# Attention and a gated MLP on one core: the second MLP product by Strassen's scheme

## Chip, core and metric

The kernel runs on one core of a Trainium2 chip. The metric is the device time of one execution in microseconds (us); lower is better. A core has five engines with a queue each, which work in order and wait for one another by semaphores: PE (TensorE, matmuls from SBUF into PSUM; its weight loads, PEld, overlap the matmuls), ACT (ScalarE), DVE (VectorE), POOL (GpSimd, which has no access to PSUM) and SP (SyncE, which here only issues DMAs). PSUM has eight banks of 512 f32 columns for 128 partitions.

## What is computed

```python
def _attn_ref(q, k, v, g_q, g_k):            # (8, 12, 448, 64) each
    ...
    q_n, k_n = (rmsnorm(q, g_q), rmsnorm(k, g_k))
    scores = scale * np.matmul(q_n, k_n.transpose(0, 1, 3, 2))
    ...
    return np.matmul(attn, v).astype(np.float32)

def _moe_ref(x, w_in, w_out):                # x: (3584, 768)
    h = x @ w_in                             # 768 -> 2048
    relu6 = np.clip(h + 3.0, 0.0, 6.0)
    g = h * relu6 / 6.0
    return (g @ w_out).astype(np.float32)    # 2048 -> 768
```

Eight sequences of 448 tokens and 12 heads go through attention with normalised queries and keys; the heads of a token, side by side, are the 768 inputs of an MLP with a gate, without residual. Inputs and output are f32, the matmuls work on bf16.

## The kernel before

**Units.** Two heads make a pair, so there are 48 pairs, six to a sequence. For a pair P, `load` brings q, k and v into slots of SBUF (slots for q and k: a ring of 6 and 2 that are used once, in space that a later stage takes over; for v likewise 6 and 2). `prep` squares q and k (ACT or POOL), sums the squares (DVE, line 454), takes the inverse root (ACT, lines 430 and 433), scales q and k into bf16 (POOL, line 369), and copies v to bf16 (`values`, on POOL, ACT or DVE). `trans` turns q and k by a DMA on SP's queue (line 561), for the first pairs on PE. `score` makes the scores on PE (line 594) and their exponentials on ACT (line 600), `av` the product with v (line 680), `finish` divides by the row sums (DVE, lines 696 and 699) and turns the result into `xT` by a DMA on SP's queue (line 706).

**The MLP.** When a sequence's six pairs are through, `h_group` computes 128 of the 2048 hidden columns of its 448 tokens: six matmuls of 448 columns (line 772), then on ACT a relu into `ts` (line 731), and on DVE the gate, which reads `ts` and PSUM and writes a row of `gT` in bf16 (line 734). `gT` holds the hidden values with the hidden index on partitions: two buffers of two sequences each (`gT_r`), so that one group of two sequences can be read while the next is written. `y_group` computes 128 tokens of the output: for each half of 384 output columns 16 matmuls that use a block of `gT` as weights and a row block of `w_out_sb` as the moving operand (line 794), all into one PSUM bank, then a copy into a row of the ring `y` (ACT, line 350, or DVE, line 352) and the store (SP's queue, line 815). Two sequences make seven such token tiles; in all there are 28, each 32 matmuls. The last tile's second half is computed in two quarters, so that its copies and stores overlap.

**PSUM.** Two tiles `S` of two banks and a tile `X` of two banks serve the scores and attention; the two banks `M` alternate for `h_group` and `y_group`. Only when attention is over do the MLP's groups get five banks.

**Order.** The program is first written down as a list of steps (`Plan.add`: what kind, which engines may do it, what it reads and writes). `ORDER` is a fixed list that says in which order the steps are issued, and `WAY` says for single steps which of their possible engines does them (0, the first, unless named). `mix` decides only which tiles of the output go beside which hidden columns, and `ORDER` then places every step. In each engine's queue the steps run in that order, whatever comes late.

Of the kernel before, what the change touches and what calls it, by code (L numbers as in the profile page):

```python
# [12 lines left out]
A_MIN = mybir.AluOpType.min  # L13
LN = mybir.ActivationFunctionType.Ln
# [152 lines left out]
]  # L167


# [36 lines left out]
def kernel(  # L206
# [11 lines left out]
    nc = tc.nc  # L218
# [743 lines left out]
```

## Time and profile before

| | |
|---|---|
| times of three runs | 422.86, 424.26, 471.55 us, median 424.26 |
| span of the profiled execution | 421.4 us |
| busiest engine | PE 413.0 us |
| other engines, busy | ACT 288.3, DVE 233.1, POOL 168.8 us |
| mean granted clock of PE | 0.999 |
| HBM read, written | 50.23 MB, 11.01 MB |

The span runs from the first to the last instruction of one execution. A group row of the profile reads: line, engine, operation, what it writes <- what it reads (partitions x elements and type), the count, then busy us and the mean ns of one, then the idle time of the engine just before these instructions and what ended it. Matmuls are pipelined: their durations overlap, and their spacing has to be read from the starts in the timeline. Some matmul records are missing from a trace (here the page shows 3959, the program has 3960).

### The profile page before, as it was taken

How to read it: one execution, taken by the hardware profiler on the slowest of the kernel's cores; microseconds unless marked ns; L12 is line 12 of the kernel's file. 1: busy time of each engine (PE TensorE's matmuls, PEld its weight loads, DVE VectorE, ACT ScalarE, POOL GpSimd, SP SyncE). 2: the span in 40 equal slices, each digit the busy share in tenths (PEclk: the TensorE clock that was granted, in tenths of full speed). 3: DMA queues.
4: the chain of work that ended last, by engine and by line, in shares of the span. 5: the costliest groups of instructions: out<-in, count | busy, mean ns of one | idle time of the engine just before them, and what ended most of it. 6: DMA issues, size and time to landing. Idle time of an engine off the chain costs nothing.

```text
span 421.4 us, 9981 instructions
## 1 busy us (share of the span) xinstructions
PE 413.0 (98%) x3959; PEld 243.8 (58%) x3960; DVE 233.1 (55%) x474; ACT 288.3 (68%) x527; POOL 168.8 (40%) x189
## 2 busy tenths in 40 slices
PE   7899999999999999999999999999999999999996
PEld 3566886555545555555555555555655556555565
DVE  5987776588875667536554754447345333333210
ACT  6999887678887988788767876677765662133201
POOL 3999596478374554427344143043210100000000
PEclk9999999999999999999999999999999999999999
DMA  7999999999779799568495683747350601120034
GB/s 241 319 282 196 258 216 177 275 268 271 178 194 252 193 252 242 111 154 211 115 224 160 164 206 73 135 154 166 82 93 12 143 2 47 30 81 27 8 107 114
DMA packets 98979, 67.77 MB, mean 161 GB/s; under 512 B 53204, under 2 KB 95476, under 8 KB 98932
## 3 DMA queue, kind: packets, MB, share of 16 engines
q1 hardware_dynamic: 93296, 60.50, 56.9%
q0 software_dynamic: 5248, 6.29, 9.0%
q8 instruction: 31, 0.51, 0.5%
q10 hardware_dynamic: 388, 0.34, 0.3%
q14 instruction: 16, 0.13, 0.1%
HBM read 50.23 MB, written 11.01 MB: 145 GB/s over the span
## 4 chain that ended last, share of the span: by engine, by line
PE 82%; DMA 7%; ACT 5%; DVE 2%; issue 1%; POOL 1%; SPq 1%; POOLq 0%; ACTq 0%; DVEq 0%
PE M L772 27%; PE M L794 25%; PE X L680 9%; PE S L594 5%; PE M L753 4%; DMA qk<-in_k_dram 4%; PE S L794 4%; PE X L594 3%; DMA T<-qks 2%; PE X L772 1%; ACT sq L364 1%; DMA out_dram<-y 1%; ACT eT L600 1%; ACT eT L622 1%; PE S L617 1%
## 5 line engine op out<-in xcount | busy, mean ns | idle before, releaser
L794 PE MATMUL M<-w_out_sb,gT 128*128 128x384 bf16 x752 | 139.3, 326 | 0.2 <-DMA w_out_sb<-in_moe_w_out_dram 0.2
L772 PE MATMUL M<-xT,w_in_sb 128*128 128x448 bf16 x618 | 135.0, 353 | 0.1
L369 POOL TENSOR_TENSOR qks<-qk,rs 112x512 bf16<-112x512 f32 (+1 forms) x91 | 91.0, 1019 | 107.3 <-ACT rs L433 77.2
L794 PEld LDWEIGHTS <-gT 128*128 128x128 bf16 x912 | 84.5, 98 | 59.5 <-issue 7.6
L734 DVE SCALAR_TENSOR_TENSOR gT<-ts,M 128x448 bf16<-128x448 f32 x119 | 73.2, 616 | 72.1 <-ACT ts L731 71.6
L600 ACT ACTIVATE eT<-S 112x896 bf16<-112x896 f32 x112 | 100.3, 915 | 15.7 <-PE S L594 8.5
L731 ACT ACTIVATE ts<-M 128x448 f32<-128x448 f32 x119 | 64.7, 545 | 42.7 <-PE M L772 29.2
L772 PEld LDWEIGHTS <-w_in_sb 128*128 128x128 bf16 x672 | 60.2, 98 | 56.3 <-issue 10.5
L366 POOL TENSOR_TENSOR sq<-qk 112x512 f32<-112x512 f32 (+1 forms) x57 | 58.0, 1024 | 52.9 <-DMA qk<-in_q_dram 29.7
L680 PEld LDWEIGHTS <-eT 112*128 112x128 bf16 x1344 | 52.7, 97 | 14.5 <-issue 2.0
L600 ACT ACTIVATE eT<-X 112x896 bf16<-112x896 f32 x56 | 51.3, 917 | 13.3 <-PE X L594 12.2
L680 PE MATMUL X<-va,eT 112*128 112x65 bf16 x1344 | 56.0, 194 | 0.1
L454 DVE TENSOR_REDUCE ssq<-sq 112x16 f32<-112x1024 f32 x42 | 50.9, 1213 | 6.1 <-POOL sq L366 4.7
L594 PE MATMUL S<-T 64*128 64x448 bf16 x224 | 34.0, 353 | 0.1
L352 DVE COPY y<-M 128x384 f32<-128x384 f32 x26 | 14.5, 556 | 30.9 <-PE M L794 30.8
L699 DVE TENSOR_TENSOR xn<-X,rd 112x512 bf16<-112x512 f32 x42 | 28.9, 689 | 1.3 <-DVE rd L696 0.2
L696 DVE RECIPROCAL rd<-X 112x8 f32<-112x8 f32 x42 | 8.6, 206 | 34.5 <-PE X L680 28.6
L594 PEld LDWEIGHTS <-T 64*128 64x128 bf16 x336 | 12.9, 94 | 24.5 <-issue 17.2
L364 ACT ACTIVATE sq<-qk 112x512 f32<-112x512 f32 (+1 forms) x40 | 23.0, 586 | 2.8 <-DMA qk<-in_k_dram 2.5
L350 ACT COPY y<-M 128x384 f32<-128x384 f32 x21 | 10.0, 477 | 19.4 <-PE M L794 19.2
L753 PE MATMUL M<-xT,w_in_sb 128*128 128x224 bf16 x192 | 22.9, 259 | 0.0
L794 PE MATMUL S<-w_out_sb,gT 128*128 128x384 bf16 (+1 forms) x128 | 22.6, 316 | 0.0
(87 smaller groups left out, 300.9 us busy)
## 6 DMA issues: line engine op xcount, KB each, us to landing
qk<-in_k_dram SPq DMA_DIRECT2D x45, 256.0 KB, 4.8
qk<-in_q_dram SPq DMA_DIRECT2D x45, 256.0 KB, 4.7
vf<-in_v_dram SPq DMA_DIRECT2D x43, 256.0 KB, 4.8
w_in_sb<-in_moe_w_in_dram POOLq DMA_DIRECT2D x4, 768.0 KB, 8.4
w_out_sb<-in_moe_w_out_dram POOLq DMA_DIRECT2D x4, 768.0 KB, 9.5
out_dram<-y SPq DMA_DIRECT2D x7, 336.0 KB, 3.5
out_dram<-y SPq DMA_DIRECT2D x8, 288.0 KB, 3.3
out_dram<-y SPq DMA_DIRECT2D x8, 240.0 KB, 2.8
```

Of the source, the lines that this page charges most:

```text
L366: em(nc.gpsimd.tensor_tensor(out=out, in0=in_, in1=in_, op=A_MULT))
L369: em((nc.vector if e == DVE else nc.gpsimd).tensor_tensor(out=out, in0=in_, in1=by.unsqueeze(3).to_broadcast(list(in_.shape)), op=A_MULT))
L454: em(nc.vector.tensor_reduce(out=ssq[:].rearrange("p i n -> p (i n)"), in_=sq[:].rearrange("p i (n d) -> p (i n) d", d=D), axis=AX_X, op=A ...
L594: em(nc.tensor.matmul(out=ps[:, a, 0:S], lhsT=qkT[r, S + t * TP:S + t * TP + 128], rhs=qkT[r, 0:S], start=True, stop=True))
L600: em(nc.scalar.activation(out=eT[:, t, 0:S2].rearrange("p (a s) -> p a s", a=2), in_=ps[0:TP, :, 0:S], func=EXP, bias=0.0, scale=1.0))
L680: em(nc.tensor.matmul(out=X_ps[:, a, i * E1:(i + 1) * E1], lhsT=eT[:, t, c:c + 128], rhs=va[:, a, t, :], start=(t == 0 and i == 0), stop=( ...
L699: em(nc.vector.tensor_tensor(out=xn[:].rearrange("p i a d -> p a i d"), in0=view()[:, :, :, 0:D], in1=rd[:].unsqueeze(3).to_broadcast([TP, ...
L731: em(nc.scalar.activation(out=ts[:], in_=ps()[:, 0:S], func=RELU, bias=0.5, scale=1.0 / 6.0))
L734: em(nc.vector.scalar_tensor_tensor(out=out, in0=shape(ts[:]), scalar=1.0, in1=shape(ps()[:, 0:S]), op0=A_MIN, op1=A_MULT))
L753: em(nc.tensor.matmul(out=ps()[:, f * SH:(f + 1) * SH], lhsT=w_in_sb[:, kt, f0:f0 + 128], rhs=xT[:, kt, z * SH:(z + 1) * SH], start=(kt == ...
L772: em(nc.tensor.matmul(out=ps()[:, 0:S], lhsT=w_in_sb[:, kt, f * 128:(f + 1) * 128], rhs=xT[:, kt, :], start=(kt == 0), stop=(kt == NKT - 1)))
L794: em(nc.tensor.matmul(out=ps()[:, 0:nc0], lhsT=gT[:, f, i * 128:(i + 1) * 128], rhs=w_out_sb[:, f, c0:c0 + nc0], start=(f == 0), stop=(f = ...
```

## The change

The output product is taken by Strassen's scheme for all token tiles from the fourth on. Two token tiles (rows i1, i2), the two halves of the 2048 hidden values and the two halves of the 768 output columns make a 2 x 2 by 2 x 2 product of blocks. Each block product is 8 matmuls of 384 columns. With A for the blocks of `gT` and B for those of `w_out`, `y_pair` forms seven products:

```diff
+    def y_pair(g, i1, i2, nb):
+        row1, row2 = y_row(False), y_row(True)
+        c11, c12, c21, c22 = half(row1, 0), half(row1, 1), half(row2, 0), half(row2, 1)
+        k = [bank(nb), bank(nb)]
+        a6 = gsum(g, 0, (i2, 0), (i1, 0), A_SUB, None)
+        a7 = gsum(g, 1, (i1, 1), (i2, 1), A_SUB, None)
+        a11, a22 = raw(g, i1, 0), raw(g, i2, 1)
+        product(k[0], (a11, B12))
+        y_copy(c22, k[0])
+        product(k[1], (a22, B21))
+        y_add(c22, k[1])
+        a5 = gsum(g, (i1, 1), (i1, 0), (i1, 1), A_ADD, None)
+        a2 = gsum(g, (i2, 0), (i2, 0), (i2, 1), A_ADD, None)
+        product(k[0], (a5, B22), start=False)
+        y_copy(c12, k[0])
+        product(k[1], (a2, B11), start=False)
+        y_copy(c21, k[1])
+        aS = gsum(g, (i1, 0), (i1, 0), (i2, 1), A_ADD, None)
+        yield 4
+        k = bank(nb)
+        product(k, (aS, BSUM))
+        y_add(c22, k)
+        y_sub(c11, c22, c12)
+        y_sub(c22, c22, c21)
+        yield 1
+        k = bank(nb)
+        product(k, (a7, B7))
+        y_add(c11, k)
+        y_store(g, i1, row1, (0, DM))
+        yield 1
+        k = bank(nb)
+        product(k, (a6, B6))
+        y_add(c22, k)
+        y_store(g, i2, row2, (0, DM))
+        yield 1
```

`gsum` is one addition or subtraction of 128 x 1024 bf16 on DVE or POOL, into one of two buffers `ga` or in place over rows of `gT`. `y_add` adds a PSUM product to half a row of y (DVE), `y_sub` subtracts two halves in SBUF (POOL or DVE), `product` is 8 matmuls. With `start=False` a product goes on in a bank that still holds the former one, after that has been copied or added out. There are 11 pairs. The first three tiles stay as they were (`y_plain`), three tiles without a partner (`y_single`) take 32 matmuls and one `gsum`.

`wsums` forms, once, three sums of blocks of `w_out` in a new tensor `wb` and replaces two blocks of `w_out_sb` by differences, in ten steps of 128 x 1536 bf16 on DVE or POOL:

```diff
+            for n, (o, x, y, op, reads, writes) in enumerate((
+                    (wb[:, 1, lo], b11, b12, A_ADD, [rl], [("wb", 1, j)] + OVER_W),
+                    (wb[:, 2, lo], b21, b22, A_ADD, [rh], [("wb", 2, j)] + OVER_W),
+                    (b12, b12, b22, A_SUB, [rl, rh, ("wb", 1, j)], [("w12", j)]),
+                    (b21, b21, b11, A_SUB, [rl, rh, ("wb", 2, j)], [("w21", j)]),
+                    (wb[:, 0, lo], b11, b22, A_ADD, [rl, rh], [("wb", 0, j)] + OVER_W))):
```

For the space, `gT` becomes one tensor of three sequences instead of two buffers of two, with the odd sequences in the middle, and the rings of input slots get shorter. Until pair 16 the space of `wb` holds three more slots for q and k and three for v:

```diff
-    NQK, NV, NSQ, NRS, NQS, NVA, NT, NE, NXN, NXT, NTS, NY = 5, 5, 2, 4, 3, 4, 4, 2, 2, 2, 2, 3
-    NQX = 2
-    qk_r = ring(NQK + 1, [128, 2, 2, T * D], FP32, "qk")
-    vf_r = ring(NV + 1, [128, 2, T * D], FP32, "vf")
+    NQK, NV, NSQ, NRS, NQS, NVA, NT, NE, NXN, NXT, NTS, NY = 5, 4, 2, 4, 3, 4, 4, 2, 2, 2, 2, 3
+    NG, NC, HF = 3, 2, NFT // 2
+    NQX, NVX, NQW, NVW, PX = 1, 2, 3, 3, 16
+    qk_r = ring(NQK, [128, 2, 2, T * D], FP32, "qk")
+    vf_r = ring(NV, [128, 2, T * D], FP32, "vf")
...
-    gT_r = ring(2, [128, NFT, S2], BF16, "gT")
+    GW = NG * S + PAD
+    gT = const.tile([128, NFT, GW], BF16, name="gT")
+    ga_r = ring(NC, [128, HF, 128], BF16, "ga")
+    wb = const.tile([128, 3, HF, HALF], BF16, name="wb")
```

The load of v now goes out a pair later than that of q and k (`load(P + 8, (0, 1))`, `load(P + 7, (2,))`). `ORDER` and `WAY` are new; PE's first 110 steps, ACT's first 56 and DVE's first 62 are of the same kinds in the same order as before (they lie in the first sequence's attention), and all later ones are placed anew. Beside the new steps, this moves copies of v from DVE and ACT to POOL and some squares from POOL to ACT.

More of the change, by code (lines that the diff above doesn't have):

```diff
@@ new lines, in gsum, with rows, f_s @@
+    def gsum(g, o, x, y, op, res):
+        def rows(i, k):
+            return gT[:, k * HF:(k + 1) * HF, g_tile(g, i):g_tile(g, i) + 128]
+        out = ga_r[o][:] if isinstance(o, int) else rows(*o)
+        wr = [("ga", o)] if isinstance(o, int) else [r for f in raw(g, *o)[1] for r in f]
+        def f_s(e):
+            em((nc.vector if e == DVE else nc.gpsimd).tensor_tensor(out=out, in0=rows(*x), in1=rows(*y), op=op))
+        plan.add("ga", [DVE, POOL], f_s, [r for t in (x, y) for f in raw(g, *t)[1] for r in f], wr)
+        if isinstance(o, int):
+            return [ga_r[o][:, f] for f in range(HF)], [[("ga", o)]] * HF
+        return raw(g, *o)
@@ new lines, with y_row, half, y_copy @@
+    yx = [0]
+    def y_row(single):
+        if not single:
+            return y_r[1], 1
+        yx[0] += 1
+        return y_r[2 * (yx[0] % 2)], 2 * (yx[0] % 2)
+    def half(yrow, n, c0=0, nc0=HALF):
+        return yrow[0][:, n * HALF + c0:n * HALF + c0 + nc0], ("y", yrow[1], n)
+    def y_copy(dst, bk, nc0=HALF):
+        def f_c(e):
+            copy(e, dst[0], bk[0]()[:, 0:nc0])
+        plan.add(f"cy{nc0}", [ACT, DVE], f_c, [bk[1]], [dst[1]])
+    def y_add(dst, bk):
+        def f_a(_):
+            em(nc.vector.tensor_tensor(out=dst[0], in0=bk[0]()[:, 0:HALF], in1=dst[0], op=A_ADD))
+        plan.add("yt", [DVE], f_a, [bk[1], dst[1]], [dst[1]])
@@ new lines, in y_sub, with f_a, y_store, f_o @@
+    def y_sub(dst, x, y):
+        def f_a(e):
+            em((nc.vector if e == DVE else nc.gpsimd).tensor_tensor(out=dst[0], in0=x[0], in1=y[0], op=A_SUB))
+        plan.add("yu", [POOL, DVE], f_a, [x[1], y[1]], [dst[1]])
+    def y_store(g, i, yrow, cols, final=False):
+        p0 = 0
+        for b, c, m in rows_of(g, i):
+            while m:
+                t, r = divmod(c, TP)
+                n = min(TP - r, m)
+                def f_o(eng, b=b, t=t, r=r, n=n, p0=p0):
+                    rows = out[b * S:(b + 1) * S, :].rearrange("(p t) n -> t p n", t=T)[t, r:r + n]
+                    em((nc.scalar if eng == ACT else nc.sync).dma_start(
+                        out=rows[:, cols[0]:cols[1]], in_=yrow[0][p0:p0 + n, cols[0]:cols[1]]))
+                plan.add(f"st{cols[1] - cols[0]}", [ACT if final and p0 else SP], f_o,
+                         [("y", yrow[1], h) for h in range(2) if cols[0] < (h + 1) * HALF and cols[1] > h * HALF], [])
+                c, m, p0 = c + n, m - n, p0 + n
@@ new lines, in y_plain @@
+    def y_plain(g, i, nb):
+        row = y_row(True)
+        for n in range(2):
+            k = bank(nb)
+            for h in range(2):
+                rr = ("w12" if n and not h else "w21" if h and not n else "w_out")
+                product(k, (raw(g, i, h), ([wcol(h * HF + f, n) for f in range(HF)],
+                                           lambda j, rr=rr, h=h: [(rr, j + 2 * h if rr == "w_out" else j)])), start=not h)
+            y_copy(half(row, n), k)
+            yield 2
+        y_store(g, i, row, (0, DM))
@@ new lines, in y_single @@
+    def y_single(g, i, nb, final):
+        row = y_row(True)
+        aS = gsum(g, 0, (i, 0), (i, 1), A_ADD, None)
+        a1, a2 = raw(g, i, 0), raw(g, i, 1)
+        for n, cols in enumerate([[(0, HALF)], [(0, HALF // 2), (HALF // 2, HALF // 2)] if final else [(0, HALF)]]):
+            for c0, nc0 in cols:
+                k = bank(nb)
+                product(k, (a1, B12) if n else (a2, B21), c0=c0, nc0=nc0)
+                product(k, (aS, B22 if n else B11), start=False, c0=c0, nc0=nc0)
+                y_copy(half(row, n, c0, nc0), k, nc0)
+                if final:
+                    c = n * HALF + c0
+                    y_store(g, i, row, (c, c + nc0), True)
+            yield 2
+        if not final:
+            y_store(g, i, row, (0, DM))
@@ L883 @@
             trans_first(P, 0, 1)
-            for n in range(P + 6, min(P + 8, NPAIR + 6)):
-                load(n)
+            if P < 4:
+                load(P + 5)
+                load(P + 6)
+            else:
+                load(P + 5, (0, 1))
     for c in range(NFT // 2):
```

223 lines of the change are left out of this document (131 added, 92 removed), and 284 rows, old and new, of tables (ORDER, WAY).

## The prediction

> **What bounds the kernel now.** I read the page of the profiled execution first: the busy shares, then the busy tenths in 40 slices with the granted clock, then the chain of work that ended last.
>
> ```profile
> span 421.4 us, 9981 instructions
> PE 413.0 (98%) x3959; PEld 243.8 (58%) x3960; DVE 233.1 (55%) x474; ACT 288.3 (68%) x527; POOL 168.8 (40%) x189
> PE   7899999999999999999999999999999999999996
> PEclk9999999999999999999999999999999999999999
> PE 82%; DMA 7%; ACT 5%; DVE 2%; issue 1%; POOL 1%; SPq 1%; POOLq 0%; ACTq 0%; DVEq 0%
> ```
>
> TensorE (PE) is busy in every slice but the first two and the last, at full clock, and 82% of the chain is its matmuls. No other engine is over 68%. The next view, the groups of instructions, names what the matmuls are; the timeline gives the true pitch, because "mean ns of one" (326) is the latency of pipelined matmuls and not their spacing.
>
> ```profile
> L794 PEld LDWEIGHTS <-gT 128*128 128x128 bf16 x912 | 84.5, 98 | 59.5 <-issue 7.6
> ...
> 396.55 2.76 PE L794 MATMUL S<-w_out_sb,gT 128*128 128x384 bf16 x16
> 399.14 0.81 PE L794 MATMUL X<-w_out_sb,gT 128*128 128x384 bf16 x4
> ```
>
> Line 794 is the product that the change rewrites; it loads weights 912 times, once per matmul. Sixteen of them start at 396.55 and the next group at 399.14: (399.14 - 396.55) / 16 = 0.162 us each. The rest of the span has to be known stage by stage, since a faster PE helps only where PE sets the pace. Windows (start, then busy us of PE, weight load, DVE, ACT, POOL, then clock, DMA share, GB/s) and the chain between 68 and 100 us:
>
> ```profile
> 80.00:100.00 20.00, 19.84 (x202) 10.77 (x200) 17.32 (x36) 16.72 (x32) 15.09 (x16) 1.00 1.18 262
> 100.00:120.00 20.00, 20.00 (x197) 10.26 (x195) 16.61 (x34) 18.34 (x34) 12.59 (x14) 1.00 0.76 195
> 380.00:400.00 20.00, 20.00 (x118) 11.29 (x116) 6.40 (x11) 6.12 (x12) 0.00 (x0) 1.00 0.03 7
> ...
> 74.49 4.37 DMA qk<-in_k_dram
> 79.85 6.71 DMA qk<-in_k_dram
> 90.76 7.17 DMA T<-qks
> 99.23 0.73 PE M L772 x3
> ```
>
> Up to about 99 us the chain runs through input loads and their preparation, with the DMA engines full; from 99 us on PE has no idle time that the windows show. From there a matmul less is 0.162 us less, as long as its operands come in time.
>
> **The change part by part.** *Matmuls removed.* A pair of token tiles takes 2 x 32 = 64 matmuls of 384 columns today and seven products of 8, so 56, afterwards. There are 11 pairs; three tiles at the start and three single tiles keep 32 each. So 11 x 8 = 88 matmuls go, all after 120 us (the first pair follows the second sequence's scores), hence inside the stage that PE bounds: 88 x 0.162 = 14.3 us. No matmul of another kind is added, and the weight loads keep their number per matmul.
>
> *Work added on DVE and POOL.* Counted in the changed program: 58 sums of gated rows (128 x 1024 bf16), 36 on DVE and 22 on POOL; 44 additions of a PSUM product to a row of y (384 columns), all on DVE; 22 subtractions between halves of y, 10 on DVE, 12 on POOL; 10 weight sums of 1536 columns, 5 on each. The rows nearest to them:
>
> ```profile
> L454 DVE TENSOR_REDUCE ssq<-sq 112x16 f32<-112x1024 f32 x42 | 50.9, 1213 | 6.1 <-POOL sq L366 4.7
> L699 DVE TENSOR_TENSOR xn<-X,rd 112x512 bf16<-112x512 f32 x42 | 28.9, 689 | 1.3 <-DVE rd L696 0.2
> L655 DVE TENSOR_TENSOR xn<-XF,rd 112x256 bf16<-112x256 f32 x12 | 4.9, 417 | 0.2
> L352 DVE COPY T<-S 128x448 bf16<-128x448 bf16 x7 | 2.7, 386 | 1.2 <-PE S L542 1.0 <-PE XF L664 0.2
> L352 DVE COPY gT<-M 128x224 bf16<-128x224 bf16 x12 | 3.2, 263 | 0.1
> L348 DVE TENSOR_SCALAR_CACHE_REDUCE va<-vf 112x512 bf16<-112x512 f32 x22 | 15.0, 681 | 1.9 <-DMA vf<-in_v_dram 1.8
> L352 DVE COPY y<-M 128x384 f32<-128x384 f32 x26 | 14.5, 556 | 30.9 <-PE M L794 30.8
> L369 POOL TENSOR_TENSOR qks<-qk,rs 112x512 bf16<-112x512 f32 x86 | 88.1, 1043 | 101.2 <-ACT rs L433 71.1 <-DMA T<-qks 17.3 <-issue 12.7
> L369 POOL TENSOR_TENSOR qks<-qk,rs 112x256 bf16<-112x256 f32 x5 | 3.1, 614 | 6.1 <-ACT rs L433 6.1
> ```
>
> A DVE sum of two bf16 rows is not in the trace. The bf16 copies rise from 263 to 386 ns over 224 elements (0.55 ns each), which carried on to 1024 gives 386 + 576 x 0.55 = 0.70 us; a 1024-element pass at the f32 rate is the reduction, 1.21 us. I take 0.70, since the operands are bf16 and contiguous as in the copies, and keep 1.21. The y addition reads f32 from PSUM like the 689 and 417 ns rows (1.06 ns per element): 0.417 + 128 x 0.00106 = 0.55 us, as the f32 copy. On POOL 256 elements more cost 0.43 us, so a sum is 1.04 + 2 x 0.43 = 1.90, at most 2 x 1.04 = 2.08 us; a subtraction 0.61 + 0.21 = 0.83; a weight sum about 2.8.
>
> DVE adds 36 x 0.70 + 54 x 0.55 + 5 x 0.98 = 59.8 us. It loses 6 copies of y (0.56 each), and 12 copies of v that the new order gives to others at about 0.68: 11.5 us. So 233 + 48 = 281 us, or 300 with sums at 1.21: 69 to 73% of 410. POOL adds 22 x 1.90 + 12 x 0.83 + 5 x 2.8 = 66 us, takes 15 v copies and gives up 10 squares, about even: 169 + 66 = 235 us, 57%. ACT gives five copies of y and three of v away and takes those ten squares, which leaves it near its 288. No engine comes near PE's 398, so the additions cost nothing as throughput. What can cost is lateness.
>
> *New handovers.* In a pair, the first four of the seven products keep both M banks of PSUM for themselves: a bank's partial sum is copied or added into y, and PE then goes on accumulating in the same bank. Between the two uses of one bank stands at least the other bank's product, 8 x 0.162 = 1.30 us; the reader takes 0.55. In the new order eleven of the returns have only that product between them, so some 0.75 us is left for two semaphore hops and whatever DVE is in the middle of. That can be a reduction of 1.21, and then PE waits up to 0.5 us: 0 to 11 x 0.5 = 5.5 us. I take 1.5, because DVE is free or in a short instruction more often than in a reduction, and today's gate and bank handovers are as tight and leave no idle time in the windows. Behind a late addition on DVE stand the next gates, and for those PE's next hidden products wait.
>
> *The end.* After the last hidden product 35 matmuls of the remaining pairs (5.7 us) run before the first that needs its gate. In that time DVE has an addition, two subtractions, two gates (0.617 each, 616 in the row below), an addition, and a sum: 0.55 x 4 + 0.62 x 2 + 0.70 = 4.1 us, from about 0.8 us on (the first addition's product has to end first). That fits; with sums at 1.21 the three in-place sums that follow come up to 1.5 us late. Bounds 0 and 2, taken 1.0, since the cover is thin and POOL's sums sit in the same chain. The final tile still ends on a 192-column copy and a store, like today.
>
> ```profile
> L734 DVE SCALAR_TENSOR_TENSOR gT<-ts,M 128x448 bf16<-128x448 f32 x119 | 73.2, 616 | 72.1 <-ACT ts L731 71.6
> qk<-in_k_dram SPq DMA_DIRECT2D x45, 256.0 KB, 4.8
> T<-qks SPq DMA_TRANSPOSE x35, 3.9
> SPq L425 <- POOL qks L369: 37.7, 7, 14.8
> ```
>
> *Slots and loads.* q/k slots go from 6 (and 2 used once) to 5, plus 1 used once and 3 in the space of the weight sums until pair 16; v slots from 6 and 2 to 4, plus 2 and 3. Up to pair 16 the loads can run further ahead, in just the stage whose chain is loads: between 0 and -1.5 us, taken 0. After it a load waits for POOL's scale of the pair five before it; on the SP queue the transposes and stores stand behind it. That wait is in today's trace already (last row: 37.7 us in 7 waits). A pair's way from load to scores is about 4.8 + 1.0 + 1.2 + 2.1 + 3.9 = 13 us, and five slots last five pairs of (421 - 99) / 42 = 7.7 us, 38 us. Covered; 0. The ten weight sums are queued where PE works between some 83 and 133 us, 5 x 0.98 on DVE and 5 x 2.8 on POOL. In the two windows from 80 to 120 us DVE had 2.7 + 3.4 us free and POOL 4.9 + 7.4, so this fits barely and can push preparation steps back: 0 to 3, taken 0, together with the loads' gain that I also leave at 0.
>
> *Sum.* -14.3 + 1.5 + 1.0 = -11.8 on a span of 421.4: 409.6. The page gives no time of its own for that execution; of the three times shown two lie close, 422.86 and 424.26, which is 1.5 and 2.9 above the span, and the third (471.55) is left aside. Against the median 424.26 the sum gives 412.5.
>
> **The rivals.** *1. Sums that shut out POOL.* The 51 DVE instructions with two SBUF inputs (36 + 10 + 5) would take turns with POOL's instructions instead of running beside them. Today's program has one DVE instruction of the kind, while POOL sat idle until 7.61:
>
> ```profile
> 5.53 0.69 DVE L369 TENSOR_TENSOR qks<-qk,rs 112x512 bf16<-112x512 f32 x1
> 7.61 0.61 POOL L369 TENSOR_TENSOR qks<-qk,rs 112x256 bf16<-112x256 f32 x1 [6.13 <-ACT rs L433]
> ```
>
> So nothing here speaks for or against it. With POOL busy 57% of the time in instructions of 1.0 to 1.9 us, one of the 51 would wait 0.57 x 0.7 = 0.4 us on average, 20 us in all: DVE still under 75%, but at the tight handovers and in the end stage, where nine DVE sums and six POOL sums alternate, about 0.4 us per pair reaches PE: 11 x 0.4 = 4.4, so 417. Chance 0.2. The Trainium skill, "SBUF — State Buffer", section "Who interferes with whom", states such a rule: a DVE instruction with two SBUF inputs contends with a GpSimd instruction that reads SBUF, and the loser blocks for the whole instruction. No run here shows it yet.
>
> *2. Slower: POOL's sums stand in the path of every pair.* POOL runs in order, and 22 sums queue behind scales of 1.04 us each. If in each pair one sum comes late by two scales and its own 1.90, less the cover that the order gives, say 2.5 us, PE loses 11 x 2.5 = 27.5: 424.3 - 14.3 + 27.5 = 437. Each pair saves 8 x 0.162 = 1.30 us, so from 1.30 us of stall per pair the change loses, and from 2.07 by over 2%. Against it: most sums are issued 2 to 5 us of PE work ahead of their product, and POOL is 57% busy. Chance 0.12.
>
> *3. The saved matmuls uncover ACT.* In the 100 to 120 us window ACT works 18.34 of 20 us. If exponentials set the pace wherever PE gets shorter, half the gain goes: 418. Against it: ACT falls to 6.12 of 20 at the end, and the average is 70%. Chance 0.06.
>
> **How the numbers follow.** Forecast 412.5 with chance 0.62: 408.5 without any stall and with the early loads' 1.5, about 416 with the upper bound of either the handovers or the weight sums. The range is 408.5 to 421: it takes in rivals 1 and 3, and leaves out rival 2 (0.12) and some 0.06 below. Two per cent is 8.5 us, about what a measurement of this kernel can tell from no change, so faster by over 2% means under 415.8: 0.64, the forecast and a little of rival 1. Within 2%: 0.24. Slower by over 2%: 0.12.
>
> **What would show it.** Right: matmuls of the second product 824 instead of 912, PE still without idle time after 100 us, sums near 0.70 us on DVE. Rival 1: DVE sums, or POOL scales, far longer than alone, when they overlap. Rival 2: PE rows waiting for POOL sums, over 1.3 us per pair. Wrong altogether: PE idle in the middle stages, or a span over 421.

## The result, and the profile after

| | before | after |
|---|---|---|
| median of the runs taken together | 424.18 us | 427.51 us |
| ratio after / before, 95% interval | | 1.0098 (1.0075 to 1.0122) |
| span of the profiled execution | 421.4 us | 426.0 us |
| mean granted clock of PE | 0.999 | 0.984 |

The forecast was 412.5 us (408.5 to 421). The changed kernel takes 1% longer than the kernel before it, and 15 us longer than forecast. Here and below, ratios leave out runs that are more than 1.5% above the fastest run of the same kernel (of the kernel before, the one of 471.55 us). The page of the changed kernel (span, busy shares, PE and its clock in 40 slices of 10.65 us, shares of the chain that ended last):

```profile
span 426.0 us, 9977 instructions
...
PE 404.6 (95%) x3872; PEld 236.7 (56%) x3872; DVE 295.7 (69%) x539; ACT 290.2 (68%) x530; POOL 247.0 (58%) x233
...
PE   8985999999958999999999999999999999999996
...
PEclk9996999999996999999999999999999999999999
...
PE 68%; DVE 10%; DMA 6%; ACT 5%; issue 4%; SPq 3%; POOL 3%; POOLq 0%; DVEq 0%; ACTq 0%
```

PE's matmul records fell from 3959 to 3872, but its row has two holes that it did not have, in the fourth slice (32 to 43 us) and the twelfth and thirteenth (117 to 138 us). In the fourth and thirteenth the clock row falls too. PE's share of the chain went from 82% to 68%.

To see where the time went I count *lost time*: the start of a matmul minus the spacing, at full clock, of all matmuls ahead of it. The spacings are read from the trace of before (0.162 us for 384 columns, as in the prediction, the other widths likewise), and the same table is used for every run below, so that its differences are idle time and time at a lower clock. The spacing of the narrow matmuls varies; taking it otherwise moves a difference in one column by up to 1 us, and the difference of the sums hardly.

| lost us | 0-30 | 30-60 | 60-120 | 120-140 | 140 to the last matmul | sum |
|---|---|---|---|---|---|---|
| before | 8.7 | 2.1 | 3.2 | 0.8 | 7.1 | 21.9 |
| after | 8.1 | 11.4 | 1.6 | 9.5 | 10.0 | 40.7 |

The 14.3 us of matmuls are gone as forecast, and 18.8 us of lost time came: the last matmul starts 4.5 us later (422.5 against 418.0). 9.3 of it lies in 30 to 60 us and 8.7 in 120 to 140 us. The view of waits for PE (line waited for: us in total, times, longest) and the windows around the two holes (busy us of PE, weight load, DVE, ACT, POOL, then clock, DMA share, GB/s) say the same:

```profile
PE M L812 <- DVE gT L768: 6.5, 2, 6.4
PE XF L698 <- DVE xn L689: 2.9, 1, 2.9
PE S L651 <- ACT eT L656: 1.8, 1, 1.8
PE S L576 <- ACT eT L656: 1.2, 1, 1.2
```

```profile
30.00:36.00 6.00, 1.32 (x16) 0.87 (x17) 3.09 (x4) 5.08 (x13) 5.74 (x6) 0.96 1.12 327
36.00:43.00 7.00, 5.83 (x75) 4.35 (x74) 5.24 (x13) 5.15 (x11) 4.57 (x6) 0.55 1.18 244
...
124.00:128.00 4.00, 0.00 (x0) 0.00 (x0) 4.00 (x1) 0.30 (x2) 4.00 (x2) 0.95 0.88 222
128.00:135.00 7.00, 5.33 (x19) 1.81 (x19) 5.37 (x8) 2.27 (x3) 0.54 (x1) 0.54 0.01 3
```

In the kernel before, PE was busy nearly all the time, at full clock, in both places:

```profile
30.00:35.00 5.00, 4.59 (x80) 3.58 (x76) 3.74 (x14) 5.00 (x10) 4.98 (x6) 1.00 1.09 259
...
120.00:140.00 20.00, 20.00 (x197) 11.63 (x198) 12.20 (x21) 15.68 (x30) 9.58 (x11) 1.00 1.09 273
```

PE idles 5.9 us in three pieces in the first hole (the last three rows of the waits) and 6.4 us at one blow in the second. Behind each, for some 7 us, the granted clock is about 0.55: PE looks busy there and does half the work.

**The second hole** in the timeline (start us, us, engine, line, operation, out<-in; the idle time before it in brackets):

```profile
121.42 1.04 POOL L403 TENSOR_TENSOR qks<-qk,rs 112x512 bf16<-112x512 f32 x1
...
121.84 7.25 DVE L868 TENSOR_TENSOR ga<-gT 128x1024 bf16<-128x1024 bf16 x1
...
122.42 6.12 POOL L837 TENSOR_TENSOR w_out_sb<-w_out_sb 128x1536 bf16<-128x1536 bf16 x2
129.01 0.61 DVE L768 SCALAR_TENSOR_TENSOR gT<-ts,M 128x448 bf16<-128x448 f32 x1
...
129.67 1.28 PE L812 MATMUL M<-xT,w_in_sb 128*128 128x448 bf16 x3 [6.38 <-DVE gT L768]
```

The first sum of gated rows on DVE takes 7.25 us. It starts while POOL scales, POOL then runs two weight differences of 3.1 us back to back, to 128.54, and the sum ends 0.55 us behind them, at 129.09. The gate behind it in DVE's queue is what PE waits for.

**The first hole:**

```profile
30.93 0.63 ACT L398 ACTIVATE sq<-wb 112x512 f32<-112x512 f32 x1 [2.73 <-DMA wb<-in_k_dram]
...
31.46 0.90 ACT L656 ACTIVATE eT<-S 112x896 bf16<-112x896 f32 x1
...
32.41 0.37 PE L651 MATMUL S<-gT 64*128 64x224 bf16 x4 [1.81 <-ACT eT L656]
...
32.91 2.35 DVE L488 TENSOR_REDUCE ssq<-sq 112x16 f32<-112x1024 f32 x2 [3.03 <-ACT sq L398]
...
35.65 0.37 PE L698 MATMUL XF<-identity,xn 112*128 112x112 bf16 x2 [2.87 <-DVE xn L689]
```

ACT's queue has the square of a pair that is loaded into the space of the weight sums; the load has not landed, ACT waits 2.73 us, and the exponentials of the first sequence stand behind it. DVE's reduction waits for the square, and the normalisation that PE needs stands behind the reduction.

The other terms of the forecast in the groups (busy us, mean ns of one, idle before):

```profile
L888 PEld LDWEIGHTS <-gT 128*128 128x128 bf16 x592 | 54.5, 98 | 41.0 <-issue 7.2 <-DVE gT L868 0.6 <-POOL sq L400 0.4
...
L868 POOL TENSOR_TENSOR gT<-gT 128x1024 bf16<-128x1024 bf16 x12 | 26.0, 2174 | 25.5 <-DVE ga L868 23.4 <-PE S L888 1.9
...
L868 DVE TENSOR_TENSOR ga<-gT 128x1024 bf16<-128x1024 bf16 x15 | 21.8, 1452 | 0.3 <-PE S L888 0.3
L888 PEld LDWEIGHTS <-ga 128*128 128x128 bf16 x232 | 21.5, 98 | 14.5 <-issue 1.5 <-DVE ga L868 0.2
L912 DVE TENSOR_TENSOR y<-M,y 128x384 f32<-128x384 f32 x37 | 20.5, 555 | 17.7 <-PE M L888 11.9 <-POOL y L917 2.3 <-ACT eT L634 2.2
L868 DVE TENSOR_TENSOR gT<-gT 128x1024 bf16<-128x1024 bf16 x21 | 20.2, 965 | 0.5 <-POOL ga L868 0.3
...
L837 POOL TENSOR_TENSOR w_out_sb<-w_out_sb 128x1536 bf16<-128x1536 bf16 x3 | 9.2, 3089 | 2.4 <-PE M L888 2.4
L917 POOL TENSOR_TENSOR y<-y 128x384 f32<-128x384 f32 x7 | 7.3, 1048 | 5.8 <-DVE y L917 4.3 <-DVE y L386 1.2 <-ACT y L384 0.2
```

592 + 232 = 824 weight loads of the second product. The y addition takes 0.555 us as forecast (0.55), POOL's sum 2.17 (1.90), its weight difference 3.09 (2.8), its y subtraction 1.05 (0.83). The DVE sums stand out: 1.45 and 0.97 us on average against 0.70.

### The profile page after: what moved, and what is told of

The parts are those of the page before. It is cut to its first block, busy times and chain, and to the rows that moved or that the text cites. A ratio compares the mean times of both kernels' runs of the same rounds, so it can differ in the third digit from the quotient of the medians.

```text
span 426.0 us, 9977 instructions
## 1 busy us (share of the span) xinstructions
PE 404.6 (95%) x3872; PEld 236.7 (56%) x3872; DVE 295.7 (69%) x539; ACT 290.2 (68%) x530; POOL 247.0 (58%) x233
## 4 chain that ended last, share of the span: by engine, by line
PE 68%; DVE 10%; DMA 6%; ACT 5%; issue 4%; SPq 3%; POOL 3%; POOLq 0%; DVEq 0%; ACTq 0%
PE M L812 23%; PE M L888 18%; PE X L714 7%; PE S L628 5%; PE M L793 4%; PE S L888 3%; DVE ga L868 3%; PE X L628 2%; SPq L459 2%; DMA out_dram<-y 2%; ACT eT L656 2%; POOL qks L403 2%; DMA qk<-in_k_dram 2%; DMA wb<-in_k_dram 2%; ACT sq L398 1%
## 5 line engine op out<-in xcount | busy, mean ns | idle before, releaser
L403 POOL TENSOR_TENSOR qks<-qk,rs 112x512 bf16<-112x512 f32 (+1 forms) x83 | 85.3, 1045 | 47.7 <-ACT rs L467 36.5
L634 ACT ACTIVATE eT<-S 112x896 bf16<-112x896 f32 x112 | 101.1, 917 | 13.3 <-PE S L628 12.3
L888 PEld LDWEIGHTS <-gT 128*128 128x128 bf16 x592 | 54.5, 98 | 41.0 <-issue 7.2
L888 PE MATMUL M<-w_out_sb,gT 128*128 128x384 bf16 (+1 forms) x392 | 70.9, 325 | 0.7 <-DVE gT L768 0.7
L400 POOL TENSOR_TENSOR sq<-qk 112x512 f32<-112x512 f32 (+1 forms) x42 | 43.3, 1036 | 27.4 <-DVE ssq L488 8.5
L868 POOL TENSOR_TENSOR gT<-gT 128x1024 bf16<-128x1024 bf16 x12 | 26.0, 2174 | 25.5 <-DVE ga L868 23.4
L868 POOL TENSOR_TENSOR ga<-gT 128x1024 bf16<-128x1024 bf16 x10 | 22.1, 2217 | 30.9 <-DVE gT L768 18.5
L912 DVE TENSOR_TENSOR y<-M,y 128x384 f32<-128x384 f32 x37 | 20.5, 555 | 17.7 <-PE M L888 11.9
L888 PEld LDWEIGHTS <-ga 128*128 128x128 bf16 x232 | 21.5, 98 | 14.5 <-issue 1.5
L888 PE MATMUL M<-wb,ga 128*128 128x384 bf16 x152 | 28.7, 326 | 0.0
L398 ACT ACTIVATE sq<-qk 112x512 f32<-112x512 f32 (+1 forms) x47 | 27.3, 594 | 1.7 <-DMA qk<-in_k_dram 1.5
L628 PEld LDWEIGHTS <-T 64*128 64x128 bf16 x336 | 12.5, 94 | 25.4 <-issue 19.1
```

Source lines behind the costliest of these rows:

```text
L398: em(nc.scalar.square(out=out, in_=in_))
L400: em(nc.gpsimd.tensor_tensor(out=out, in0=in_, in1=in_, op=A_MULT))
L403: em((nc.vector if e == DVE else nc.gpsimd).tensor_tensor(out=out, in0=in_, in1=by.unsqueeze(3).to_broadcast(list(in_.shape)), op=A_MULT))
L628: em(nc.tensor.matmul(out=ps[:, a, 0:S], lhsT=qkT[r, S + t * TP:S + t * TP + 128], rhs=qkT[r, 0:S], start=True, stop=True))
L634: em(nc.scalar.activation(out=eT[:, t, 0:S2].rearrange("p (a s) -> p a s", a=2), in_=ps[0:TP, :, 0:S], func=EXP, bias=0.0, scale=1.0))
L868: em((nc.vector if e == DVE else nc.gpsimd).tensor_tensor(out=out, in0=rows(*x), in1=rows(*y), op=op))
```

## The experiments

Two theories for the two holes, with rivals, were put to 16 kernels. The table has what each run left (e4 is not a whole kernel and has no row); a ratio is to the kernel before, run beside it, with its 95% interval; the lost time is counted as above, from one profiled run each; "half clock" is the time at half clock between 10 and 415 us.

| run | median us | ratio | lost 30-60 | lost 60-120 | lost 120-140 | half clock us |
|---|---|---|---|---|---|---|
| after | 427.51 | 1.0098 (1.0075 to 1.0122) | 11.4 | 1.6 | 9.5 | 13.7 |
| e1 | 422.39 | 0.9959 (0.9945 to 0.9973) | 10.8 | 1.6 | 3.3 | 6.8 |
| e2 | 434.20 | 1.0230 (1.0196 to 1.0264) | 17.4 | 1.5 | 8.6 | 27.3 |
| e3 | 427.53 | 1.0075 (1.0055 to 1.0096) | 17.2 | 1.3 | 1.9 | 20.5 |
| e5 | 447.35 | 1.0574 (1.0519 to 1.0628) | 16.0 | 6.8 | 10.3 | 23.9 |
| e6 | 422.87 | 0.9990 (0.9972 to 1.0008) | 11.9 | 2.3 | 3.1 | 10.2 |
| e7 | 422.72 | 0.9986 (0.9968 to 1.0004) | 11.6 | 1.3 | 2.9 | 10.2 |
| e8 | 431.29 | 1.0170 (1.0151 to 1.0189) | 6.0 | 12.3 | 1.2 | 10.2 |
| e9 | 424.70 | 1.0019 (1.0005 to 1.0033) | 6.2 | 5.2 | 2.4 | 3.4 |
| e10 | 424.49 | 1.0032 (1.0002 to 1.0062) | 6.7 | 4.7 | 2.0 | 10.2 |
| e11 | 423.80 | 1.0009 (0.9988 to 1.0029) | 7.2 | 8.7 | 1.8 | 10.2 |
| e12 | 423.02 | 0.9984 (0.9965 to 1.0003) | 7.8 | 4.2 | 2.9 | 10.2 |
| e13 | 420.93 | 0.9954 (0.9899 to 1.0009) | 4.8 | 12.8 | 1.9 | 6.8 |
| e14 | 432.68 | 1.0207 (1.0150 to 1.0263) | 5.3 | 17.3 | 2.2 | 10.2 |
| e15 | 418.30 | 0.9866 (0.9842 to 0.9889) | 5.2 | 5.0 | 2.0 | 0.0 |
| e16 | 419.31 | 0.9900 (0.9870 to 0.9930) | 6.6 | 4.6 | 2.1 | 0.0 |

e13's six runs spread from 420.1 to 427.8 us. Its median and ratio are those of the three lower ones (420.05, 420.93, 425.19), so its interval is wide; its lost time and half clock are those of the longest, 427.83 us, which is the one that was profiled.

### The second hole: e1, e4, e7

**e1**: two steps of `WAY` back to DVE, the first engine of their list.

```diff
-    671: 1, 743: 2, 770: 1, 774: 1, 775: 1, 776: 1, 777: 1, 796: 1, 805: 1, 830: 1, 862: 1, 888: 1, 895: 1,
+    671: 1, 743: 2, 770: 1, 774: 1, 777: 1, 796: 1, 805: 1, 830: 1, 862: 1, 888: 1, 895: 1,
```

> The two differences of the output weights (3.1 us each, back to back on POOL at 122.4 to 128.5 us) are computed by DVE, at the same places of the order; all else as in the changed kernel. Theory P (a DVE sum of two SBUF operands cannot run while POOL works and here lost its turn to both differences): the DVE sum that took 7.25 us at 121.84 us takes 0.7 to 1.3 us, PE's idle 6.4 us before the third h part at 129.67 us and the half-speed matmuls behind it go, and the time falls by 7 to 9 us, to 418.5 to 420.5. Rival Q (the sum was held by something else, or PE would have waited there for the sums anyway): the time stays within 2 us of 427.5. Rival R (on DVE the differences, about 1 us each, block the gates as much as they free the sum): 422 to 427.

Measured 422.39 us, 5.1 less than the changed kernel. The same sum, in the timeline of e1:

```profile
122.54 0.76 DVE L867 TENSOR_TENSOR ga<-gT 128x1024 bf16<-128x1024 bf16 x1
```

0.76 us instead of 7.25, and the lost time of 120 to 140 us falls by 6.2. Theory P holds for the sum; its price was 2 to 4 us too high, and the time is at the lower end of what rival R gave (422 to 427). R's mechanism is in the trace, but small: PE has two new waits for gates, one of 0.6 us at 130 us, where the gate stands behind a weight difference on DVE (128.96 to 129.91 us), and one of 1.1 us at 137 us behind a token sum of 1.53 us. With these two entries of `WAY` alone the kernel is 0.4% below the kernel before (0.3 to 0.6).

**e4** measures the disputed cost by itself: an ACT copy starts DVE and POOL together, DVE's operation stands behind a short one.

```diff
+    def dsum(o=ga):
+        nc.vector.tensor_tensor(out=o[:], in0=gT[:, 0:8], in1=gT[:, 8:16], op=A_ADD)
...
+    def dyadd():
+        nc.vector.tensor_tensor(out=y[:, 0:384], in0=ps[:, 0:384], in1=y[:, 0:384], op=A_ADD)
...
+        ([dsum], [pscale, lambda: pw(0), lambda: pw(1)]),
...
+        ([dcopy], [pscale, lambda: pw(0), lambda: pw(1)]),
+        ([dyadd], [pscale, lambda: pw(0), lambda: pw(1)]),
```

> Only scenes of DVE and POOL work and a store of one tile; the whole computation of the reference is left out. Each scene is run three times, started on both engines by one ACT copy, DVE behind a short operation so that POOL is already at work. Theory P: the DVE sum of two SBUF operands (128 x 1024 bf16) takes 0.7 us alone; with one POOL operation of about 1 us and one of 2.2 us in the queue it ends about 0.55 us after the first or the second of them; with two differences of 3.1 us behind the first it takes up to 7 us. If the sum always gets its turn at the next end of a POOL instruction, it never takes more than about 1.6 us, whatever stands behind, and the 7.25 us of the changed kernel have another reason. DVE's copy of one SBUF operand, the PSUM addition and the reduction: by P they run beside POOL at their own times, 0.2 to 1 us; if they are shut out too, they are as long as the sum.

The timeline of e4, in four places:

```profile
60.20 0.69 DVE L58 TENSOR_TENSOR ga<-gT 128x1024 bf16<-128x1024 bf16 x1 [0.26 <-ACT sm L103]
...
98.95 1.04 POOL L70 TENSOR_TENSOR qs<-qf,go 112x512 bf16<-112x512 f32 x1
...
99.33 8.28 DVE L58 TENSOR_TENSOR ga<-gT 128x1024 bf16<-128x1024 bf16 x1 [0.26 <-ACT sm L103]
99.95 3.08 POOL L76 TENSOR_TENSOR w<-w 128x1536 bf16<-128x1536 bf16 x1
...
102.99 1.03 POOL L70 TENSOR_TENSOR qs<-qf,go 112x512 bf16<-112x512 f32 x1
103.99 3.08 POOL L76 TENSOR_TENSOR w<-w 128x1536 bf16<-128x1536 bf16 x1
...
153.43 3.98 DVE L61 COPY ga<-gT 128x1024 bf16<-128x1024 bf16 x1 [0.26 <-ACT sm L103]
...
162.67 0.56 DVE L64 TENSOR_TENSOR y<-ps,y 128x384 f32<-128x384 f32 x1 [0.45 <-ACT sm L108]
163.10 3.08 POOL L76 TENSOR_TENSOR w<-w 128x1536 bf16<-128x1536 bf16 x1
```

With POOL idle the sum takes 0.69 us, what the forecast took. Started into a POOL operation it waits past three ends of POOL instructions and ends at 107.61, 0.54 us behind the fourth (103.99 + 3.08 = 107.07). So the 7.25 us need nothing else to explain them, and the statement that the sum gets its turn at the next end falls. The addition with one operand in PSUM keeps its 0.56 us beside POOL; a copy of one bf16 operand in SBUF does not (3.98; 0.43 at another place of the run). There the expectation missed: by P the copy was to run at its own time. The short scaling of 256 bf16 elements that stands ahead of each scene's operation was shut out too (6.17 us at 53.77; 0.28 at 70.44). The Trainium skill, "SBUF — State Buffer", section "Who interferes with whom", states that a DVE instruction with two SBUF inputs contends with a GpSimd instruction that reads SBUF, and that the loser blocks for the whole instruction. The rows agree, and go further: one instruction can lose several times in a row.

**e7**: every sum, difference and weight sum of the seven products on DVE.

```diff
-    671: 1, 743: 2, 770: 1, 774: 1, 775: 1, 776: 1, 777: 1, 796: 1, 805: 1, 830: 1, 862: 1, 888: 1, 895: 1,
+    671: 1, 743: 2, 796: 1, 805: 1, 830: 1, 862: 1, 888: 1, 895: 1,
-    962: 1, 990: 1, 994: 1, 998: 1, 1026: 1, 1042: 1, 1043: 1, 1074: 1, 1075: 1, 1100: 1, 1107: 2, 1127: 1,
+    962: 1, 963: 1, 994: 1, 1026: 1, 1027: 1, 1042: 1, 1043: 1, 1074: 1, 1075: 1, 1100: 1, 1107: 2, 1127: 1,
...
```

The rows further on change likewise: 22 token sums lose their 1 (POOL), 12 differences of y get one (DVE).

> The changed kernel with every sum and difference that the seven products need on DVE: its 22 token sums (2.2 us each), 12 differences of y (1.0 us) and 5 weight sums (3.1 us) leave POOL; order as in the changed kernel. Theory P (what is left of the loss behind 140 us is DVE sums shut out by POOL's): at least e1's gain, and up to 2 us more, 419.5 to 422.5. Theory D (DVE, with 29 us more work on top of 292, becomes late for the gates): 424 or more, and PE's idle behind gates grows over the whole span.

422.72 us, between what the two theories gave and no better than e1 (ratio 0.9986 against 0.9959). Taking POOL's remaining 2.2 us sums away and putting 29 us more on DVE gains nothing together; the two effects were not measured apart. So the excess of the other DVE sums over 0.68 us (about 11 us in all in the changed kernel) is probably hidden; the one sum behind two 3.1 us instructions was not.

### The first hole, by moving steps: e2, e3, e6

**e2** moves six squares behind the exponentials that they stood ahead of; **e3** is e1 and e2 together.

```diff
-    386, 317, 318, 310, 347, 270, 254, 495, 255, 348, 385, 360, 367, 319,
+    317, 318, 310, 347, 270, 254, 495, 255, 348, 360, 367, 319, 361, 341,
```

> Six squares (ACT, steps 385, 386, 488, 523, 524, 553, pairs loaded into the space of the weight sums) and what hangs on them are moved behind the exponentials and copies of the first sequence that they stood ahead of; no work is left out. Theory S (ACT's queue stood at 30.9 us behind a square whose load had not landed, and DVE's behind its reduction, so PE idled 5.9 us between 30 and 42 us at a lowered clock): PE's idle there goes and the time falls by 6 to 9 us, to 418.5 to 421.5. Rival T (the loads themselves are late, or the moved normalisation is then late for the second sequence): the first attention product against V starts as late as before the edit (48.8 us), or PE idles between 76 and 120 us instead, and the time stays within 2 us of 427.5.

> Both edits at once: the two weight differences on DVE, and the six squares later. If P and S hold and the two losses are independent, the gains add up: 427.5 - 8.7 - 8.9 = 410, range 408.5 to 413, which is 3% less than the kernel before the change. If one stall only hid behind the other, the gain is that of the larger one alone: 418 to 421.

434.20 and 427.53 us, outside all that was expected: e2 is 6.7 us slower than the changed kernel, e3 5.1 slower than e1. The chain of e2 shows the wait one step further on, at a copy of v in DVE's queue:

```profile
22.39 5.30 DMA wb<-in_v_dram
27.69 0.02 issue
27.71 5.91 DMA wb<-in_v_dram
33.62 0.02 issue
33.64 0.04 DVE va L381
```

Theory S named the right wait and the wrong cure: with the squares out of the way the next step with a load that has not landed holds the queue, and the squares now hold up the second sequence (PE's waits of 1.8 and 1.6 us at 48 and 51 us are for DVE copies behind reductions that waited for a square).

**e6**: as many pairs under way as in the kernel before.

```diff
-    NQX, NVX, NQW, NVW, PX = 1, 2, 3, 3, 16
+    NQX, NVX, NQW, NVW, PX = 1, 2, 2, 2, 16
```

> e1 with two input slots instead of three for queries with keys, and for values, in the space of the weight sums, so that as many pairs are under way as in the kernel before (eight); five loads move behind the release of a slot, nothing else. Theory L (loads at 30 to 38 us beyond the eighth pair slow the weights and the next inputs): 416 to 420. Theory O (order of the steps): within 1.5 us of e1's 422.4, since the steps that stall at 31 to 42 us wait for loads that were issued before 31 us in both kernels.

422.87, within 0.5 us of e1, and the lost time of 30 to 60 us stays (11.9): the depth of the prefetch is not the cause.

### The first hole, by a new order: e5, e8 to e12

These are e1 with early steps in another order; e5 puts the kernel before's order on the new steps, the others come from a search over a model with in-order queues, durations from these traces and the rates of the two DMA queues (which e5's model lacked). The edits are long lists; the first row of e8 and of e11 for the others:

```diff
-    44, 95, 45, 82, 87, 221, 105, 96, 129, 88, 46, 19, 122, 228,
+    228, 120, 44, 95, 87, 121, 96, 45, 229, 245, 46, 88, 122, 47,
```

```diff
-    312, 239, 335, 204, 196, 313, 205, 240, 238, 303, 250, 206, 304, 314,
+    335, 313, 204, 238, 196, 250, 303, 267, 337, 304, 359, 305, 1, 312,
```

> The two weight differences on DVE as in e1, and the first 900 of the 2487 steps in another order: the order of the kernel before for its first 45 us of PE work, adapted by small moves to the slots and dependencies of the changed kernel, with the engine of 12 early steps changed. Same work. Theory O (the early stall is one of the new order: which step stands ahead of which while loads, exponentials and normalisations of the first sequence run): e1's lost time between 30 and 60 us, 9 us more than the kernel before, falls to 2 to 4, and the time is 414 to 418. Theory L (the loads of the changed kernel, deeper and together with the weights, are what is late): it stays within 2 us of e1's 422.4.

> e1 (the changed kernel, its two weight differences on DVE) with its first 1,100 steps, about the first 150 us, in another order on every engine, the input loads' queue among them: the order is from a search over a model of queues, measured durations and the two DMA queues' measured rates. Same engines, same slots, same work. Theory O (the early stalls are a matter of the order, and can be had back): between 30 and 60 us the lost time is 3 to 6 us less than e1's, and the time is 414 to 419. Theory I (seven products leave PE short of work that is ready while the first sequences are still being normalised, whatever the order): 421 to 424.

> As e8, but the search began from the kernel before's order of the first 45 us, and 12 early squares, copies and casts keep the engine that they had there. Theory O: 413 to 419. Theory I: 421 to 424. If it is over 425, the model lacks what made e5 slow, and an order from it proves nothing.

> As e8, but with the queue of loads and stores and the issues of the weight loads in the changed kernel's own order: only the steps on PE, ACT, DVE and POOL stand otherwise. If the order of the loads is what is late (theory L): no gain, 421 to 424, where e8 gains. If it is the steps that stand ahead of others on ACT and DVE (theory O): within 2 us of e8.

> e1 with only the 400 steps between about 26 and 78 us in another order, on all engines and the queue of loads; before and behind them every step stands as in the changed kernel. Theory O: the lost time of 30 to 60 us (10.8 in e1, 2.2 in the kernel before, 6.0 to 6.7 in e8 to e10, which lost as much again between 10 and 30 us) falls to 6 to 8, and the time is 418 to 420. Theory I: 421.5 to 424.

> As e11, with the loads' queue untouched. Theory O: within 1 us of e11, 418 to 421. Theory L (the loads' order): e11 gains and this one does not, 422 to 424.

e5 is a miss: 447 us, with a load of k in its chain that takes 14.2 us while two weight loads, issued at 46.8 and 53.4 us, are under way beside it. Its two longest waits of PE are the two holes again, at other steps: 7.7 us up to 41.8 us, where a DVE reduction (40.25) stood behind a square on POOL whose load had not landed (9.6 us of waiting), and 6.5 us near 130 us, where a weight sum on DVE took 5.43 us beside two scales and a weight difference on POOL. e8 to e12 cut the lost time of 30 to 60 us to 6 to 8 us, with the loads' queue untouched (e10, e12) almost as well as with it reordered (e8, e9, e11), so theory L falls as the cause of that lost time; but none beats e1, since they lose as much elsewhere. By their times theory O missed in all five: e11 (423.80 us) came out where theory I had it, e12 (423.02) where theory L had it, e8 to e10 above both, and e10 6.8 us from e8. The windows of e12 show why a little less idle time is worth nothing:

```profile
25.00:30.00 5.00, 2.73 (x47) 1.77 (x44) 4.22 (x11) 3.61 (x7) 4.44 (x6) 0.95 1.01 341
30.00:35.00 5.00, 3.82 (x40) 2.06 (x39) 2.85 (x8) 4.24 (x8) 2.53 (x4) 0.50 1.09 349
35.00:40.00 5.00, 5.00 (x50) 3.60 (x48) 2.12 (x7) 3.21 (x7) 3.38 (x4) 0.52 1.18 246
```

PE's longest single idle time there is 1.54 us, but in these five microseconds it is busy 2.73, and then runs ten at half clock, in the last five without any idle time. What has to go is not the longest gap but every stretch in which PE is busy for half the time or less.

### The first hole, with PE kept busy: e13 to e16

The search now also punishes 3.4 us with PE busy under 82%; the first 23 us stay as in the changed kernel. 21 early steps (e14: 12) go back to the engine that they had before. e15 and e16 also take away the two places where e13 and e14 lost time.

```diff
-    299, 248, 201, 220, 226, 191, 300, 246, 192, 234, 301, 242, 193, 202,
+    191, 246, 201, 248, 242, 234, 299, 301, 202, 249, 192, 250, 343, 243,
```

> e1 with its steps between about 23 and 150 us in another order, begun from the kernel before's order and engines (21 early squares, copies and casts on the engine that they had there, five squares from ACT to POOL among them) and changed by a search that this time also punishes every 3.4 us in which PE would be busy for less than 82%; the first 23 us stand as in the changed kernel. Theory C (the early loss is idle of PE plus the half clock that follows any 3.4 us with PE busy under about half; an order that keeps PE busy there has neither): no window at half clock before 418 us, lost time between 30 and 60 us 3 to 5 us against e1's 10.8, and 414 to 417.5. Theory I (the seven products leave too little ready work there): a window at half clock between 25 and 60 us in this order too, and 421 to 425.

> The same from another start, with 12 early steps on the kernel before's engines instead of 21. Theory C: 414 to 418.5, no half clock between 20 and 418 us. Theory I: 421 to 425.

e13 and e14 lose 4.8 and 5.3 us between 30 and 60 us, with no half clock there: theory C holds for the stretch. Its times do not (414 to 417.5 and 414 to 418.5), nor its statement that no half clock comes later, for each profiled run lost more at one later place. In e13's, its longest, a transposing transfer was on its way for 15.8 us; a load of output weights had been issued just ahead of it. What e13's shorter runs lost there is not on record. e14's timeline (first row: three weight sums on DVE):

```profile
92.02 13.29 DVE L836 TENSOR_TENSOR wb<-w_out_sb 128x1536 bf16<-128x1536 bf16 x3 [0.51 <-POOL va L387]
92.95 3.09 POOL L836 TENSOR_TENSOR wb<-w_out_sb 128x1536 bf16<-128x1536 bf16 x1
95.99 2.04 POOL L402 TENSOR_TENSOR qks<-qk,rs 112x512 bf16<-112x512 f32 x2
98.00 3.08 POOL L836 TENSOR_TENSOR w_out_sb<-w_out_sb 128x1536 bf16<-128x1536 bf16 x1
```

This is the second hole again, made by another order: weight sums on DVE shut out by weight sums and scales on POOL; PE idles 9.9 us behind it.

> e13's order up to about 47 us, all ten weight sums on DVE, the last load of the output weights issued next to the one before it, and the steps of 47 to 160 us ordered anew with the transposing transfers counted on the queue that the loads use: e13 lost 6 us where such a transfer took 15.8 us, and e14 lost 10 us where a weight sum on DVE stood shut out behind five POOL operations. Theory C: lost time at 60 us as in e13 (14 to 15 us, e1 20), no stall over 2 us behind it, 415 to 419, which is 1 to 2% less than the kernel before. Theory I: 421 to 425.

> The same with the loads' queue ordered by the search too, from about 42 us on. Theory C: 415 to 419. Theory I: 421 to 425.

e15 is within what theory C gave, e16 0.3 us above it; both are below both kernels, and no single wait of PE in them is over 1.1 us. The page of e15:

```profile
span 416.7 us, 9995 instructions
...
PE   8998999999999999999999999999999999999996
...
PEclk9999999999999999999999999999999999999999
...
PE 84%; DVE 6%; DMA 4%; ACT 3%; POOL 1%; issue 1%; SPq 0%; DVEq 0%; POOLq 0%
```

PE is without a hole, the clock is full, and PE carries 84% of the chain. It does the work of the changed kernel with its slots; what differs is the order of the steps up to about 160 us, the engine of 21 early steps, and the five weight sums that moved from POOL to DVE. These were changed together, so their shares are not known; that e11 and e12, which to e1 add a new order alone, and only from 26 us on, bring the lost time of 30 to 60 us from 10.8 to 7.2 and 7.8 us (e15: 5.2) says that the order has the larger part there. So the seven products do make this kernel faster, by 1.3% (1.1 to 1.6), once the order suits them; the order that came with the change cost more than they bring. Whether the kernel before would gain from such a search too was not tried; e15's gain over it is not from idle time saved, since e15 loses more than it in the three stretches of the table.

## Why the prediction was wrong, point by point

- **Matmuls removed, 14.3 us.** Right: 824 remain, and the work of PE fell by that much. Its busy time fell by 8.4 us only (413.0 to 404.6), since it also counts the stretches at half clock.
- **Durations of the added work.** The DVE sum alone is 0.69 us (taken 0.70), the y addition 0.555 (0.55). POOL's operations were priced 10 to 26% too low. As throughput the added work fits: DVE 295.7 us (forecast 281 to 300), POOL 247.0 (235), ACT 290.2 (288).
- **Ten weight sums, "0 to 3, taken 0": the step that failed.** They were priced as filling free time of DVE and POOL ("fits barely"). What they did was to keep DVE's first token sum out for 6.6 us beyond its own 0.7: 8.7 us of lost time between 120 and 140 us, of which e1 gets 6.2 back.
- **Rival 1** named the mechanism, with the price wrong, and in its heading the direction. It had DVE and POOL take turns, 0.4 us on average, with POOL instructions of 1.0 to 1.9 us, though the prediction itself had weight sums of 2.8. DVE is shut out rather than POOL, sometimes past several ends of POOL instructions, and the cost falls on one place where two long POOL instructions follow each other. Elsewhere no cost of it shows (e7, which adds work to DVE at the same time).
- **Slots and loads up to pair 16, "between 0 and -1.5 us, taken 0": the second step that failed.** It measured 9.3 us of lost time between 30 and 60 us. The prediction looked at how many slots there are (e6: no matter) and not at which steps the new order puts ahead of the exponentials in ACT's and DVE's queues while a load is still on its way. It said that the chain up to 99 us runs through loads and preparation, and then charged the rearrangement of just that stage with nothing.
- **A term that was not in the sum: the clock.** Each hole is followed by 6.8 us at half clock. With PE busy half of that is lost, up to 3.4 us for each hole: 5.9 + 6.4 us of idle time and 2 x 3.4 make at most 19.1, against the 18.0 of lost time that came in the two stretches.
- **New handovers 1.5 and end 1.0.** The size was right in sum: the stretch from 140 us on lost 2.9 us more than before (10.0 against 7.1). Little of it is at the end: from the last hidden product to the last matmul the lost time is 0.6 us against 0.1 before, and from the last matmul to the last instruction it is 3.6 us against 3.4. The rest is spread over the stretches between, at most 1.3 us in any 20, and its waits were not followed one by one; so the split into 1.5 and 1.0 is not shown.
- **Rivals 2 and 3** did not happen: PE hardly waits for POOL's sums (no row of its waits names them), and ACT's busy time is where it was.

What came is the prediction's own sign of being wrong altogether: PE idle in the middle stages, and a span over 421. With the two holes closed (e15) the span is 4.7 us below the kernel before, not 11.8. e15 still loses 3.1 us more than before between 30 and 60 us, 3.0 between 60 and 140 and 3.2 behind that. Whether an order exists that saves the first two was not settled; e15 shows that a new order, with the engines of 26 steps, gets back 9.3 of the 16.4 us by which the span missed its forecast of 409.6.

## What to carry to other kernels

Before a sum of two SBUF operands goes to DVE, look at what POOL runs at that place: DVE's instruction can stand still until POOL pauses, with everything behind it in DVE's queue, so long SBUF operations belong on one of the two engines, not on both side by side. In e4 a bf16 copy out of SBUF was shut out in the same way. Where an order is made anew, price each step that can wait for a load by what stands behind it in its queue, not by its engine's free time. And a hole in PE costs more than its length: count the stretches in which PE is busy under half.

## What the runs showed of the hardware

- **How the clock falls.** The granted clock holds for multiples of 3.41 us. Over the traces of the two kernels and of all runs but e4, such a stretch at full clock, between 10 and 410 us, with PE busy under 45% was followed by half clock 15 times of 15, with 45 to 60% 6 of 12, and above 60% in none of nearly 1,900. Half clock then lasts 3.4 to 20 us, until PE has been busy for about a full stretch. The Trainium skill, "TensorE: Matmul & The Clock Gate", section "What's actually happening", has the clock fall after an idle window of some 3.4 us; here it also fell behind stretches in e11 and e12 with no gap over 1.8 us, so a half-idle window can be enough.
- **Who wins between DVE and POOL.** A shut-out DVE sum of 128 x 1024 ends 0.54 to 0.57 us behind the end of the POOL instruction at which it gets its turn, and POOL's next is then longer by about 0.45 us (1.48 instead of 1.04 in e4). It gets its turn at the first, second or a later end; which one, the runs do not tell.
